# Block-causal attention and a hash-routed expert layer: q, k, V and weights loaded as bfloat16 through the GpSimd queue, and a new order of head pairs

## The chip, the cores and the metric

The kernel runs on one core of one Trainium2 chip. The metric is the device time of one execution in microseconds (us), lower is better. An execution has 336.15 us around a profiled span of 334.5 us; the other runs are given below.

## The reference, cut to what matters

```python
# q, k, v: [8, 8, 576, 64] float32
scores = (1 / sqrt(64)) * q @ k.T                       # per batch and head
scores = where(block_i >= block_j, scores, -1e9)        # blocks of 64 positions
attn = softmax(scores);  o = attn @ v
x = o.transpose(0, 2, 1, 3).reshape(4608, 512)          # one row per token
expert = token_ids * 2654435761 % 8                     # 4608 int64 ids
out[expert == e] = relu(x[expert == e] @ w1[e]) @ w2[e] # w1 [8,512,1024], w2 [8,1024,512]
```

## The kernel before, in words

The program has two parts: attention over 8 batches of 4 pairs of heads (32 pairs, `g`), and 8 experts over the tokens that a hash sends to them. The order of instructions on each engine is the order in which the program is written; nothing reorders it (a manual schedule). Each engine runs its own list in order, and waits where a tile that it needs is not ready.

**Loads.** `load_qk` and `load_v` fetch a batch of q, k and V as float32, on the SP queue (k of the first batch on ACT's), in runs of 256 to 1024 bytes. `cast_qk` turns q and k to bfloat16 on DVE (L175) and their last 64 rows on POOL (L180); `cast_v` and `cast_v4` do so for V on POOL (L188 to L199), into the tiles `vx` (six key tiles per head) and `v4` (the last 64 keys). The two weight matrices of an expert are loaded on POOL's queue with a cast to bfloat16 (`load_w1`, L555, and `load_w2`, L560).

**Attention.** For a pair `g`, `T_pair` transposes q and k on PE (eight 128 x 128 transposes, L236) and DVE copies them out of PSUM into `qkT` (L241); `T_rest` does the last 64 rows of all heads of a batch (L211, L217). `S_chunk` computes the scores of both heads of a pair in three chunks of 512 columns: matmuls of 64 rows, one head in the upper and one in the lower half of the array (L248, L260), and a small matmul that adds the mask (L270); ACT then takes the exponential of the chunk in one instruction (L294) into `pt`. `S_rest` does this for the last 64 keys (L302, L307). `PV` multiplies `pt` with V and a column of ones (15 matmuls per head, L331 and L336), and `norm` on DVE divides by the sum (L348, L351) into `xs`, which `write_x` stores to DRAM as rows of x (L362, L364): on SP for the first batches, on POOL from batch 5. The steps of one pass over `g` are the first chunk of `g`, the first half of `PV(g - 2)`, the second chunk, the second half and `norm(g - 2)`, the third chunk, the transposes of `g + 2`, and casts. There are two PSUM tiles for scores, one for `O`, and two for transposes.

**Routing.** `route` computes from the token ids each token's place in its expert's list, `rows`, `place_a` (one-hot tables on DVE, L499 and L502, multiplied on POOL, L505 and L508) and `place_b` (matmuls into the PSUM tile `pq`, which is one of the two for transposes, L518, and an addition on DVE, L521) turn it into the table `perm3` of rows. `place_a(j)` stands in pass 5 + 2j, `place_b(j)` in pass 8 + 2j.

**Experts.** `gather_x` fetches 128 rows of x by `perm3` (L567, POOL queue). The first three gathers of experts 0 and 1 need only batches 0 to 5 and stand in passes 27 and 28; the others wait for all of x. Each expert takes its tiles through `transpose_x` (L683, L684), `stage_a` or, for experts 0 and 1 in two parts, `stage_a_part` (L696 or L715, with a Relu on ACT), and `stage_b` (L729), whose results DVE copies out (L734) and POOL scatters (L736).

All transfers of the POOL queue use eight semaphores in turn, so that each issue waits until the transfer eight issues earlier has landed; the queue's transfers are issued in the order of POOL's list.

Of the kernel before, what the change touches and what calls it, by code (L numbers as in the profile page):

```python
# [19 lines left out]

B, H, S, D = 8, 8, 576, 64
E, DM, FF = 8, 512, 1024
# [15 lines left out]
def kernel(  # L38
# [26 lines left out]
    maskk = const.tile([P, 2, P], BF16, name="maskk")  # L65
    maskq = const.tile([P, P], BF16, name="maskq")
# [11 lines left out]


    nc.vector.memset(maskk[:], 0.0)  # L80
    nc.vector.memset(maskq[:], 0.0)
    for m in range(2):
        row = slice(64 * m, 64 * m + 1)
        nc.vector.memset(maskk[row, 0, 96:128], NEG)
        nc.vector.memset(maskk[row, 1, 32:64], NEG)
        nc.vector.memset(maskk[row, 1, 96:128], NEG)
        nc.vector.memset(maskq[row, :], 1.0)
# [3 lines left out]
    psT = att_ctx.enter_context(tc.tile_pool(name="psT", bufs=2, space=bass.MemoryType.PSUM))  # L91
# [9 lines left out]
    def load_qk(b, h0=0, h1=H, rest=True, main=True, engs=None):  # L101
        if b not in loaded:
            loaded[b] = [ld.tile([P, 36, D], F32, name="qf", tag="qf"),
                         ld.tile([P, 36, D], F32, name="kf", tag="kf"), None]
        for w, src in ((0, q), (1, k)):
            t = loaded[b][w]
            eng = engs[w] if engs else nc.sync
            if main and w == 0:
                eng.dma_start(
                    t[:, 4 * h0 : 4 * h1, :].rearrange("p (h c) d -> p h (c d)", c=4),  # L110
                    src[b, h0:h1, 0:512, :].rearrange("h (p c) d -> p h (c d)", c=4),
                )
            elif main:
                for r in range(2):
                    eng.dma_start(
                        t[:, 4 * h0 : 4 * h1, :].rearrange(
                            "p (h r c) d -> p h r (c d)", r=2, c=2)[:, :, r],
                        src[b, h0:h1, 256 * r : 256 * r + 256, :].rearrange("h (p c) d -> p h (c d)", c=2),
                    )
            if rest:  # L120
                for g in range(2):
                    eng.dma_start(
                        t[64 * g : 64 * g + 64, 32:36, :],
                        src[b, 4 * g : 4 * g + 4, 512:576, :].rearrange("h r d -> r h d"),
                    )

    def load_v(b):
        vf = ld.tile([P, 36, D], F32, name="vf", tag="vf")
        vm = vf[:, 0:32, :].rearrange("p (h r c) d -> p h r (c d)", h=H, r=2)
        for r in range(2):  # L130
            nc.sync.dma_start(
                vm[:, :, r, :],
                v[b, :, 256 * r : 256 * r + 256, :].rearrange("h (p c) d -> p h (c d)", c=2),
            )
        for m in range(2):
            nc.sync.dma_start(
                vf[64 * m : 64 * m + 64, 32:36, :],
                v[b, :, 512:576, :].rearrange("(r m) s d -> m s r d", m=2)[m],
            )
        loaded[b][2] = vf  # L140

    casted = {}
    vexts = []
    for z in range(2):
        vx = fix.tile([P, H, 6, D + 1], BF16, name=f"vx{z}")
        v4 = fix.tile([P, NP, 2, D + 1], BF16, name=f"v4{z}")
        nc.vector.memset(vx[:, :, :, D : D + 1], 1.0)
        nc.gpsimd.memset(v4[:], 0.0)
        for m in range(2):
            nc.vector.memset(v4[64 * m : 64 * m + 64, :, m, D : D + 1], 1.0)  # L150
        vexts.append((vx, v4))
    PTW = 1536
    pts, pt4s = [], []
    for z in range(3):
        pt = fix.tile([P, 2 * PTW + 64], BF16, name=f"pt{z}")
        nc.gpsimd.memset(pt[:, 2 * PTW :], 0.0)
        pts.append(pt)
    for z in range(2):
        pt4 = fix.tile([P, NP * 64 + 64], BF16, name=f"pt4{z}")
        nc.gpsimd.memset(pt4[:, NP * 64 :], 0.0)  # L160
        pt4s.append(pt4)
# [5 lines left out]
    def cast_qk(b, which, r0=0, r1=NP, rest=True):  # L167
        src = loaded[b][which]
        cb = casted.setdefault(b, {})
        if which not in cb:  # L170
            cb[which] = att.tile([P, 36, D], BF16, name="qb" if which == 0 else "kb",
                                 tag="qb" if which == 0 else "kb")
        dst = cb[which]
        if r1 > r0:
            nc.vector.tensor_copy(  # L175
                dst[:, 8 * r0 : 8 * r1, :].rearrange("p (r c m) d -> p r m c d", c=4, m=2),
                src[:, 8 * r0 : 8 * r1, :].rearrange("p (r m c) d -> p r m c d", c=4, m=2),
            )
        if rest:
            nc.gpsimd.tensor_copy(dst[:, 32:36, :], src[:, 32:36, :])  # L180

    def cast_v(b, pr):
        vf = loaded[b][2]
        vx, v4 = vexts[b % 2]
        hs = slice(2 * pr, 2 * pr + 2)
        vm = vf[:, 0:32, :].rearrange("p (h s) d -> p h s d", h=H)
        eng = nc.vector if b == 0 and pr < 2 else nc.gpsimd
        eng.tensor_copy(vx[:, hs, 0:4, 0:D], vm[:, hs])  # L188
        if pr % 2:
            return  # L190
        hs = slice(2 * pr, 2 * pr + 4)
        nc.gpsimd.tensor_copy(vx[0:64, hs, 4:6, 0:D], vm[0:64, hs, 0::2, :])
        nc.gpsimd.tensor_copy(vx[64:128, hs, 4:6, 0:D], vm[0:64, hs, 1::2, :])

    def cast_v4(b):
        vf = loaded[b][2]
        vx, v4 = vexts[b % 2]
        for m in range(2):
            nc.gpsimd.tensor_copy(  # L199
                v4[64 * m : 64 * m + 64, :, m, 0:D], vf[64 * m : 64 * m + 64, 32:36, :])  # L200

# [3 lines left out]
    def T_rest(b):  # L205
        qk = qkTs[b]
        tp = psT.tile([P, 8, P], BF16, name="tp", tag="tp")
        for w in range(2):
            src = casted[b][w]
            for x in range(2):  # L210
                nc.tensor.transpose(  # L211
                    out=tp[:, 2 * w + x, :],
                    in_=src[:, 32 + 2 * x : 34 + 2 * x, :].rearrange("p a d -> p (a d)"),
                    identity=identbf[:],
                )
        for w in range(2):
            nc.vector.tensor_copy(  # L217
                qk[:, :, w, 512:576].rearrange("p (g x) r -> p x g r", g=2),
                tp[:, 2 * w : 2 * w + 2, :].rearrange("p x (g r) -> p x g r", g=2),
            )  # L220

    def T_pair(g):
        b, pr = divmod(g, NP)
        if pr == 0:
            qkTs[b] = att.tile([P, NP, 2, S], BF16, name="qkT", tag="qkT")
        qk = qkTs[b]
        tp = psT.tile([P, 2, 512], BF16, name="tp", tag="tp")
        for w in range(2):
            src = casted[b][w]
            for c in range(4):  # L230
                s0 = (pr * 4 + c) * 2
                if w == 0:
                    o = tp[:, 0, :].rearrange("p (i c j) -> p c i j", i=4, c=4)[:, c]
                else:
                    o = tp[:, 1, 128 * c : 128 * c + 128]
                nc.tensor.transpose(  # L236
                    out=o,
                    in_=src[:, s0 : s0 + 2, :].rearrange("p a d -> p (a d)"),
                    identity=identbf[:],
                )  # L240
        nc.vector.tensor_copy(qk[:, pr, :, 0:512], tp[:])  # L241


    def mm_pair(b, pr, ps, o0, kt, q0, n, first=False):
        qk = qkTs[b]
        for m in range(2):
            rows = slice(64 * m, 64 * m + 64)
            nc.tensor.matmul(  # L248
                ps[:, m, o0 : o0 + n],
                lhsT=qk[rows, pr, 1, 128 * kt : 128 * kt + 128],  # L250
                rhs=qk[rows, pr, 0, q0 : q0 + n],
                start=first, stop=False,
            )

    def mm_c(b, pr, ps, o0, r):
        qk = qkTs[b]
        for x in range(2):
            for m in range(2):
                rows = slice(64 * m, 64 * m + 64)
                nc.tensor.matmul(  # L260
                    ps[64 * x : 64 * x + 64, m, o0 : o0 + 128],
                    lhsT=qk[rows, pr, 1, 256 * r + 128 * x : 256 * r + 128 * x + 64],
                    rhs=qk[rows, pr, 0, 256 * r : 256 * r + 128],
                    start=False, stop=False,
                )

    def mm_mask(ps, o0, c, n, last=False):
# [53 lines left out]
    def PV(g, m):  # L321
# [4 lines left out]
        if m == 0:  # L326
            ots[g] = psO.tile([P, 2, 512], F32, name="O", tag="O")
# [260 lines left out]
    for w in range(2):  # L588
        cast_qk(0, w, 0, 0)
# [258 lines left out]
```

## Time and profile before

| What | Value |
|---|---|
| Median of 3 runs | 339.33 us (337.66 to 340.61) |
| Profiled execution | 336.15 us, of it the span 334.5 us |
| PE, DVE, ACT, POOL busy | 276.5, 152.5, 142.5, 183.4 us |
| First and last Exp | 12.10 us start, 137.07 us end |
| Second expert stage of expert 0 starts | 178.39 us |
| Granted PE clock, mean | 0.951 |

PE is the matmul engine, PEld its loads of the stationary operand, DVE the vector engine, ACT the scalar engine, POOL is GpSimd. In a row of the profile `L294 ACT ACTIVATE pt<-ps ... x96 | 94.2, 1023 | 34.4 <-PE ps L270 34.2` the count is 96, the busy time 94.2 us, the mean of one 1023 ns, and the engine stood idle for 34.4 us just before them, most of it until PE had written `ps` at L270. In a row of the timeline the first number is the start in us, the second the duration of the merged stretch, and the bracket holds the idle time before it and what ended it. In a row of busy times by stretch come the stretch and its length, the busy time and number of instructions of PE, PEld, DVE, ACT and POOL, the granted clock, the share of the DMA engines, and GB/s.

### The profile page before, as it was taken

The page shows a single profiled execution, that of the slowest core. Times are in us where ns is not written, and L with a number is a line of the kernel's source. Part 1 is how long each engine was busy: PE and PEld are TensorE (multiplying, and loading weights), DVE is VectorE, ACT ScalarE, POOL GpSimd, SP SyncE. Part 2 cuts the span into 40 slices and gives each one's busy share as a digit, 9 for nine tenths or more (in the row PEclk, how much of TensorE's full clock was granted, in tenths as well). Part 3 has the DMA queues.
Part 4 walks back from the last instruction along what each step waited for, and adds up shares of the span by engine and source line. Part 5 has one row for each costly group of instructions (what it writes and reads, how often), then busy time and mean ns, then how long its engine had stood idle before and what let it go on. Part 6 is the DMA issues. An engine that isn't in the chain of part 4 may idle for free. (4 is left out here: it accounts for less than half of the span.)

```text
span 334.5 us, 7914 instructions
## 1 busy us (share of the span) xinstructions
PE 276.5 (83%) x3247; PEld 198.3 (59%) x3247; DVE 152.5 (46%) x342; ACT 142.5 (43%) x169; POOL 183.4 (55%) x265
## 2 busy tenths in 40 slices
PE   1559898989799899458589899799897996999990
PEld 0337676767577676347476594665745845759430
DVE  6487899888878775221011413033141130240430
ACT  1337888779687978304322050330501402406000
POOL 2185867687966529682487517447175075051451
PEclk9999999999989999959869999999999898999996
DMA  7999997979897975969189998677786586537231
GB/s 195 283 290 282 261 289 203 262 199 285 203 297 203 294 197 123 205 182 184 55 179 231 180 232 221 177 138 229 151 174 187 111 177 187 109 121 148 94 135 45
DMA packets 67044, 64.54 MB, mean 193 GB/s; under 512 B 17218, under 2 KB 61060, under 8 KB 64960
## 3 DMA queue, kind: packets, MB, share of 16 engines
q0 software_dynamic: 9248, 32.73, 41.1%
q1 hardware_dynamic: 55104, 30.12, 33.7%
q10 hardware_dynamic: 2656, 1.18, 1.4%
q8 instruction: 26, 0.43, 0.5%
q14 instruction: 10, 0.08, 0.1%
HBM read 67.15 MB, written 15.20 MB: 246 GB/s over the span
## 5 line engine op out<-in xcount | busy, mean ns | idle before, releaser
L294 ACT ACTIVATE pt<-ps 128x1024 bf16<-128x1024 f32 x96 | 94.2, 1023 | 34.4 <-PE ps L270 34.2
L701 ACT ACTIVATE hT<-hp 128x640 bf16<-128x640 f32 x48 | 33.6, 704 | 95.4 <-PE hp L696 78.6
L729 PE MATMUL yp<-w2b,hT 128*128 128x512 bf16 x320 | 70.2, 379 | 0.0
L696 PE MATMUL hp<-xT,w1b 128*128 128x320 bf16 x384 | 57.4, 309 | 9.1 <-ACT hT L701 8.2
L736 POOL DMA_INDIRECT out_dram<-ysb,perm x40 | 39.8, 995 | 38.6 <-DVE ysb L734 30.0
L696 PEld LDWEIGHTS <-w1b 128*128 128x128 bf16 x384 | 52.9, 145 | 13.5 <-issue 10.2
L567 POOL DMA_INDIRECT xg<-x_dram,perm x40 | 40.8, 1020 | 23.6 <-issue 12.9
L734 DVE COPY ysb<-yp 128x512 f32<-128x512 f32 x40 | 27.7, 692 | 55.9 <-PE yp L729 49.7
L729 PEld LDWEIGHTS <-hT 128*128 128x128 bf16 x320 | 31.1, 98 | 36.2
L684 DVE COPY xT<-tpx 128x512 bf16<-128x512 bf16 x40 | 15.6, 421 | 77.4 <-PE tpx L683 75.6
L331 PE MATMUL O<-vx,pt 128*128 128x65 bf16 x896 | 41.0, 199 | 6.7 <-DVE xs L351 5.4
L331 PEld LDWEIGHTS <-pt 128*128 128x128 bf16 x896 | 33.4, 101 | 10.2 <-issue 5.2
L248 PE MATMUL ps<-qkT 64*128 64x64 bf16 (+2 forms) x384 | 36.2, 269 | 3.0 <-ACT pt L294 2.6
L351 DVE TENSOR_TENSOR xs<-O,rs 128x320 bf16<-128x320 f32 x64 | 28.4, 486 | 1.1
L270 PE MATMUL ps<-maskq,maskk 64*128 64x64 bf16 (+1 forms) x256 | 28.1, 213 | 0.0
L188 POOL CAST vx<-vf 128x512 bf16<-128x512 f32 x30 | 21.1, 707 | 9.2 <-DMA vf<-in_v_dram 5.5
L719 ACT ACTIVATE hT<-hp 128x768 bf16<-128x768 f32 (+1 forms) x16 | 11.3, 704 | 31.7 <-PE hp L715 29.9
L241 DVE COPY qkT<-tp 128x1024 bf16<-128x1024 bf16 x32 | 22.0, 687 | 5.3 <-PE tp L236 4.6
L715 PE MATMUL hp<-xT,w1b 128*128 128x384 bf16 (+1 forms) x128 | 21.9, 338 | 2.3 <-DVE xT L684 2.3
L555 POOL DMA_DIRECT2D w1b<-in_moe_w_dram x8 | 4.8, 596 | 33.7 <-PE tpx L683 33.7
L683 PE MATMUL tpx<-identbf,xg 128*128 128x128 bf16 x160 | 14.7, 229 | 10.3 <-DMA xg<-x_dram,perm 6.6
L715 PEld LDWEIGHTS <-w1b 128*128 128x128 bf16 x128 | 17.4, 149 | 6.5 <-issue 2.9
(120 smaller groups left out, 289.6 us busy)
## 6 DMA issues: line engine op xcount, KB each, us to landing
vf<-in_v_dram SPq DMA_DIRECT2D x16, 512.0 KB, 5.9
w1b<-in_moe_w_dram POOLq DMA_DIRECT2D x8, 1024.0 KB
w2b<-in_moe_w_dram POOLq DMA_DIRECT2D x8, 1024.0 KB
qf<-in_q_dram SPq DMA_DIRECT2D x7, 1024.0 KB, 8.4
kf<-in_k_dram SPq DMA_DIRECT2D x14, 512.0 KB, 7.2
x_dram<-xs SPq DMA_DIRECT2D x20, 128.0 KB
x_dram<-xs POOLq DMA_DIRECT2D x12, 128.0 KB
qf<-in_q_dram SPq DMA_DIRECT2D x16, 64.0 KB, 6.3
```

The source lines that it names most:

```text
L248: nc.tensor.matmul(ps[:, m, o0 : o0 + n], lhsT=qk[rows, pr, 1, 128 * kt : 128 * kt + 128], rhs=qk[rows, pr, 0, q0 : q0 + n], start=first, ...
L270: nc.tensor.matmul(ps[:, m, o0 : o0 + 128 * n].rearrange("p (t h j) -> p t h j", h=2, j=16)[:, :, 0, :], lhsT=maskk[rows, c, :], rhs=maskq ...
L294: nc.scalar.activation(ptv[:, :, 512 * ch : 512 * ch + 512], ps[:], ACT.Exp, scale=SCALE)
L331: nc.tensor.matmul(O[:, t, :], lhsT=pt[:, m * PTW + o0 : m * PTW + o0 + 128], rhs=vx[:, h, i, :], start=(n == 0), stop=(n == t),)
L351: nc.vector.tensor_tensor(out=xs[:, :, 0:DM].rearrange("p t (d h k) -> p h t d k", d=4, h=H)[:, h], in0=O[:, m, :, 0:D].rearrange("p t (k ...
L567: nc.gpsimd.indirect_dma_start(out=xgs[g % (2 * G)][:], out_offset=None, in_=x_dram[0:n, :], in_offset=bass.IndirectOffsetOnAxis(ap=perm3[ ...
L696: nc.tensor.matmul(hp[:, t, 0:HC], lhsT=w1b[:, db, ft::NFT], rhs=xT[:, db, t * HC : (t + 1) * HC], start=(db == 0), stop=(db == NKT - 1),)
L701: nc.scalar.activation(hT[:, ft, :].rearrange("p (t n) -> p t n", t=2), hp[:, :, 0:HC], ACT.Relu)
L715: nc.tensor.matmul(hp[:, ft - f0, 0 : P * (t1 - t0)], lhsT=w1b[:, db, ft::NFT], rhs=xT[:, db, c], start=(db == 0), stop=(db == NKT - 1),)
L729: nc.tensor.matmul(yp[:], lhsT=hT[:, ft, tt * P : (tt + 1) * P], rhs=w2b[:, ft, :], start=(ft == 0), stop=(ft == NFT - 1),)
L734: nc.vector.tensor_copy(ysb[:], yp[:])
L736: ins = nc.gpsimd.indirect_dma_start(out=out[:, :], out_offset=bass.IndirectOffsetOnAxis(ap=perm3[:, gg : gg + 1], axis=0), in_=ysb[:], in ...
```

## The change

q, k and V are loaded by the POOL queue with a cast to bfloat16 in the transfer. q and k land in a layout in which a partition holds 18 successive rows of a head, for two heads (runs of 4608 bytes in DRAM); V lands directly in `vx`, which now has four key tiles of 96 columns per head, in three copies. All casts and the float32 tiles are gone. `T_group` replaces `T_pair` and `T_rest`: 18 transposes of 128 x 64 for half of a batch's q or k, and one strided copy. Heads of a pair are now `pr` and `pr + 4`. The scores use whole key tiles (`CHUNKS`, `mm_c` is gone). `PV` trails by one pair instead of two, after both first chunks; there are two `pt` instead of three. The PSUM of the transposes is one tile of two banks, and `place_b` uses the unused end of the next `O` tile. x rows keep their order, so `write_x` is one transfer per batch and one for the rest, and `vlo` is one column. Weights: w1 of experts 0 and 1 in passes 24 and 25, w2 in 26 and 30 (before: 25, 26, 29, and after the loop). `mo` has 8 buffers instead of 10. In the diff, code that both have is left out, and so are the memsets and the definitions of tiles.

```diff
+RUN = 18
+DV = 96
+NV = 3
...
-    psT = att_ctx.enter_context(tc.tile_pool(name="psT", bufs=2, space=bass.MemoryType.PSUM))
+    psT = att_ctx.enter_context(tc.tile_pool(name="psT", bufs=1, space=bass.MemoryType.PSUM))
...
+    def load_qk(b):
+        loaded[b] = []
+        for w, src in ((1, k), (0, q)):
+            t = ld.tile([P, 2, RUN, D], BF16, name="qb" if w == 0 else "kb",
+                        tag="qb" if w == 0 else "kb", bufs=3)
+            nc.gpsimd.dma_start(
+                t[:].rearrange("p m c d -> p m (c d)"),
+                src[b].rearrange("(m h) (j c) d -> (h j) m (c d)", m=2, c=RUN))
+            loaded[b].insert(0, t)
...
+    def load_v(b):
+        vx, v4 = vexts[b % NV]
+        for i in range(NT):
+            nc.gpsimd.dma_start(
+                vx[:, :, i, 0:D], v[b, :, 128 * i : 128 * i + 128, :].rearrange("h p d -> p h d"))
+        for m in range(2):
+            nc.gpsimd.dma_start(
+                v4[64 * m : 64 * m + 64, :, m, 0:D],
+                v[b, 4 * m : 4 * m + 4, 512:576, :].rearrange("r s d -> s r d"))
...
+    def T_group(b, n, act=False, pool=None):
+        if b not in qkTs:
+            qkTs[b] = [att.tile([P, NP, S], BF16, name=x, tag=x, bufs=3) for x in ("qT", "kT")]
+        w, z = divmod(n, 2)
+        c0, n = RUN // 2 * z, RUN // 2
+        pool, tag = pool or (psT, "tp")
+        tp = pool.tile([P, 16, P], BF16, name="tp", tag=tag)
+        for c in range(n):
+            for m in range(2):
+                nc.tensor.transpose(out=tp[64 * m : 64 * m + 64, c, :],
+                                    in_=loaded[b][w][:, m, c0 + c, :], identity=identbf[:])
+        (nc.scalar.copy if act else nc.vector.tensor_copy)(
+            qkTs[b][w][:].rearrange("p r (j c) -> p (r j) c", c=RUN)[:, :, c0 : c0 + n],
+            tp[:, 0:n, :].rearrange("p c r -> p r c"))
...
+    CHUNKS = [[(0, 0, 0, 512)], [(0, 1, 128, 448), (448, 0, 512, 64)], [(0, 2, 256, 320), (320, 3, 384, 192)]]
+    MASKS = [[0], [0], [0, 320]]
...
+        for n, (o0, kt, q0, w) in enumerate(CHUNKS[ch]):
+            mm_pair(b, pr, ps, o0, kt, q0, w, first=n == 0)
+        for o0 in MASKS[ch]:
+            mm_mask(ps, o0, last=o0 == MASKS[ch][-1])
+        pt = pts[g % 2]
...
-        for t in range(NT):
-            r0 = S * b + P * t
-            eng.dma_start(
-                x_dram[r0 : r0 + P, :].rearrange("(j c) d -> c j d", c=4), xs[:, t, :])
+        eng.dma_start(
+            x_dram[S * b : S * b + 512, :].rearrange("(t p) d -> p t d", p=P), xs[:, 0:NT, :])
...
-    def place_b(b):
+    def place_b(b, g):
         ohp, ohg = places.pop(b)
-        pq = psT.tile([P, 512], F32, name="pq", tag="tp")
+        ots[g] = psO.tile([P, 2, 512], F32, name="O", tag="O")
+        pq = ots[g][:, 0, 512 - 2 * NG :]
...
+    load_qk(0)
+    load_v(0)
+    load_qk(1)
+    T_group(0, 2)
+    T_group(0, 3, act=True, pool=(psO, "O"))
+    T_group(0, 0, pool=(psS, "ps"))
+    T_group(0, 1, act=True, pool=(psS, "ps"))
+
+    Ts = {g: [] for g in range(NPAIRS + 1)}
+    for b in range(1, B):
+        for n, g in zip((2, 3, 0, 1), (2, 2, 3, 3) if b == 1 else (4 * b - 3, 4 * b - 2, 4 * b - 1, 4 * b - 1)):
+            Ts[g].append((b, n))
...
+    loads[0].append((load_v, 1))
+    for b in range(2, B):
+        loads[4 * b - 7].append((load_qk, b))
+        loads[4 * b - 5].append((load_v, b))
+    for g, what in ((24, (load_w1, 0)), (25, (load_w1, 1)), (26, (load_w2, 0)), (30, (load_w2, 1))):
+        loads[g].append(what)
+    for g in range(NPAIRS + 1):
         b, pr = divmod(g, NP)
         live = g < NPAIRS
         if live:
             S_chunk(g, 0)
             S_chunk(g, 1)
+        if g in mids:
+            place_b(mids[g], g - 1)
+        if g >= 1:
+            PV(g - 1, 0)
+            PV(g - 1, 1)
+            norm(g - 1)
         if live:
             S_chunk(g, 2)
             if pr == 0:
                 S_rest(b)
+        for bn in Ts[g]:
+            T_group(*bn)
         for step in steps[g]:
             step()
+        if pr == 0 and b >= 1:
             write_x(b - 1)
+        for load, n in loads[g]:
+            load(n)
```

In the kernel after the change the transfers of q and k are line L103, those of V L121 and L124, the transposes and copies of `T_group` L156 and L158, the matmuls of `place_b` L407.

## The prediction

> **What bounds the kernel now.** I read, in this order: the page's busy shares and its 40 slices, the busy times by stretch, the timeline of ACT and PE inside the attention loop, and the timeline where attention ends. The chain of waits is of no help: it stops after the last two scatters.
>
> ```profile
> span 334.5 us, 7914 instructions
> PE 276.5 (83%) x3247; PEld 198.3 (59%) x3247; DVE 152.5 (46%) x342; ACT 142.5 (43%) x169; POOL 183.4 (55%) x265
> 33.20:137.10 103.90, 94.36 (x1963) 71.56 (x1961) 84.30 (x183) 84.22 (x92) 73.31 (x121) 0.98 0.88 234
> 137.10:178.40 41.30, 28.21 (x218) 22.74 (x216) 6.22 (x16) 10.45 (x15) 25.56 (x30) 0.79 0.73 161
> 178.40:334.50 156.10, 134.87 (x826) 91.47 (x823) 40.41 (x75) 34.41 (x50) 69.94 (x75) 0.96 0.65 159
> ```
>
> The three stretches (busy PE, PEld, DVE, ACT, POOL, clock, DMA share, GB/s) are 28 head pairs of attention, the seam to the experts, and the experts. The change leaves the experts' code as it is, so their 156 us stay. Ahead of them lies the fill (the first Exp starts at 12.10 and the fifth pair at 33.2).
>
> ```profile
> L294 ACT ACTIVATE pt<-ps 128x1024 bf16<-128x1024 f32 x96 | 94.2, 1023 | 34.4 <-PE ps L270 34.2
> 53.85 2.86 ACT L294 ACTIVATE pt<-ps 128x1024 bf16<-128x1024 f32 x3 [0.23 <-PE ps L270]
> ...
> 58.93 0.58 PE L518 MATMUL pq<-ohg,ohp 128*128 128x144 bf16 x5 [1.31 <-DVE qkT L241]
> ...
> 59.85 1.96 ACT L294 ACTIVATE pt<-ps 128x1024 bf16<-128x1024 f32 x2 [1.89 <-PE ps L270]
> ```
>
> In the loop ACT sets the pace: three Exps back to back take 2.86 and 0.23 passes before the next, 3.09 us a pair. Once per batch PE stands at L518 for a PSUM tile that DVE must empty, and ACT then waits 1.14 to 2.31 us. 103.9 us over 28 pairs is 3.71 each.
>
> ```profile
> 148.53 0.61 POOL L560 DMA_DIRECT2D w2b<-in_moe_w_dram x1
> 162.81 1.09 POOL L567 DMA_INDIRECT xg<-x_dram,perm  x1 [10.09 <-DMA x_dram<-xs]
> 165.66 0.61 PE L683 MATMUL tpx<-identbf,xg 128*128 128x128 bf16 x4 [3.18 <-DMA xg<-x_dram,perm]
> 178.39 0.81 PE L729 MATMUL yp<-w2b,hT 128*128 128x512 bf16 x3
> ```
>
> At the seam the last rows of x are written behind a weight load in the same queue, and the gathers wait 10.09 us for them. With other gaps and a cold clock (0.79) it is 41.3 us from the last Exp to the second expert stage, for 28.2 us of busy PE.
>
> **What the Trainium skill says.** "DMA: Bandwidth & Descriptors", SWDGE vs HWDGE vs iDMA: a transfer that casts must be issued by GpSimd, whose cores write its descriptors in software; Anatomy of one DMA adds "You can emit a lot of descriptors before the incremental cost shows up". The trace agrees as far as it goes: on POOL 64 rows (L364) took 573 ns and 128 rows (L555) 596. No row here has 1024 runs. "VectorE: DVE Perf Modes", What auto-detection actually checks: two 16-bit elements a cycle need step 1. The trace has only the fast case, L241: 1024 elements in 687 ns. "TensorE: Matmul & The Clock Gate", Part 3: matmuls in different column groups of the array run side by side. Eight quadrant matmuls of 128 columns (L260) start within 0.24 us at 53.28, against 0.55 us for the eight full transposes at 53.68, which agrees, though those differ in rows too.
>
> **The change, part by part.**
>
> Casts: four DVE casts a batch (757 and 841 ns) and about 7.4 us of POOL casts a batch (59.3 us in six groups) go. They were beside ACT's work; by themselves they save nothing but DVE room.
>
> Loads: all on POOL, eight transfers a batch; each waits for the one eight before it, which has long landed. Data: k and q in runs of 4608 bytes. By the DMA records the 128 packets of a weight load (2 MiB read, 8 packets an engine) last 6.5 us, with 625 ns for the shortest packet, so 1.18 MB is 3.6 at that pace and 2.8 at that packet's; V is 4608 runs of 256 bytes, at 19 ns each (the mean of the old 256-byte packets) over 16 engines 5.5 us. With the x rows some 13 us a batch, under the batch's 17: hidden. Descriptors: I take 0.54 us plus 0.9 ns a run, between the 0.4 of L364 against L555 and the 2.6 of L364 against L362 (737 ns, 128 rows in another order). A V transfer of 1024 runs is then 1.5 us (0.95 to 3.2), a batch 4.3 + 5.1 = 9.4 us of POOL (5120 runs); with the two L392/L395 products of 1.58 and a memset or two about 13.5 of 17 us. Hidden, with little to spare.
>
> Fill: k then q now land whole, at about 6 and 9 us; two groups of transposes and a copy on ACT (1152 elements; by ACT's 512, 768 and 1024 rows 1.13 us) put the first Exp near 12.3 instead of 12.10. No step gain there.
>
> Transposes: eight plus one of 58 ns a pair become 18 with 64 columns. If they overlap as L260's do, 0.6 us a pair, if not 1.0; I take 0.6. Their copy reads PSUM with a step of 128 elements, so one element a cycle: 1152 / 0.96 = 1200 plus the 150 ns that L351 has over its 320 elements, 1.35 us, four a batch. Bounds: 0.75 (L241's rate) and 1.6.
>
> Scores: 28 matmuls a pair become 18 (the third chunk 0.68 to about 0.40 us). PV stays at 30 (0.57 per 15). PE per pair: 0.36 + 0.36 + 1.14 + 0.40 + 0.6 = 2.86 us, under ACT.
>
> Order: PV now trails by one pair, behind both first chunks. From the second chunk's start: PV ends at 1.50, the third chunk at 1.90, its Exp runs 2.10 to 3.12, and the next second chunk, which needs that PSUM tile, starts at 3.17. So 3.17 a pair; 3.53 with S_rest; place_b adds 0.3, but its wait for the shared tile is gone (four or five stalls, 8.5 us).
>
> What is late next: the last two transposes of a batch (q) stand at the end of the pair before their use, with one PSUM tile between them. Third chunk ends 1.90; transposes to 2.5; copy, behind the 1.13 us norm on DVE, to about 4.1; transposes to 4.7; copy to 6.1; only then the next batch's first chunk, whose second starts at 6.6 to 7.1. So 3.9 us more than a plain pair, with ACT idle, at seven boundaries, and 2.3 more at the first, where k's two groups share a pair.
>
> Sum: a middle batch is 3.53 + 2.86 + 3.17 + 3.2 + 3.9 = 16.7; with place_b in two pairs (four batches) 17.3; the first 19.0; the last 12.8. 19.0 + 2 x 16.7 + 4 x 17.3 + 12.8 = 134.4. The same recurrence gives the loop before 100.9 where the trace has 103.9, so times 1.03: 138.4. From 12.3 the last Exp ends at 150.7, against 137.07: 13.6 us later.
>
> Seam: w1 and w2 go out from pair 24 on, three loads of 6.5 us in the 21 us before pair 30 and the fourth after; x's last rows are written with nothing before them, and the late gathers land while PE does the early parts. What remains: PV and norm 2.7; two times tiles 1.9 (155.19 to 157.09) and 32 matmuls 5.35; two times 1.24 (173.60 to 174.84) and 3.6. 26.9 us instead of 41.3: 14.4 gained. Against it, a pause of 3.7 us of norm (L348, released by nothing the trace names) near the end of attention before may recur: 1.5. Small edits (route, rows, masks, memsets) lie beside loads: nothing either way, at most 1 us.
>
> Together 13.6 - 14.4 + 1.5 = +0.7 us. The profiled execution is 336.15 (1.65 around its span); on the median of 339.33 that is 340.0.
>
> **Rivals.** (1) POOL becomes the bound, the case on the slow side: descriptors of V at L121. A batch fits as long as 4.3 + 5.12 s + 4.2 stays under 17.3, s below 1.7 ns a run. At 2.0 PE waits 8 us in all (348), at 2.6 31 us (371). For it: L362's 737 ns, the indirect transfers' 1020 ns for 128 rows, the eight short runs per partition. Against it: 596 ns for 128 runs. (2) The column halves don't overlap: 18 transposes in 1.0 us; plain pairs 3.26, boundaries 0.4 more: 154.0 rather than 147.1 before the 3 per cent, 347. For it: all 58 ns rows are full width. (3) The strided copy keeps L241's rate: 0.75 us, the boundary stall falls to 2.5 us and the batch to 16: 10 us earlier, 329.5. Against it: step 128, and runs of nine with odd starts.
>
> **How the numbers follow.** The forecast has 0.45, with 333 to 347 of its own from the bounds (clock, fill, 1.5 us of pause, w loads): of it 0.07 faster, 0.25 within, 0.13 slower, at the 1% that a measurement of this kernel can tell. Rival 1 has 0.27 (0.26 slower, 0.01 within), rival 2 0.16 (0.12 slower, 0.04 within), rival 3 0.12, faster. Faster 0.19, within 0.30, slower 0.51. The range reaches from rival 3 to most of rival 1: 330 to 366.
>
> **What would show it.** Right: an ACT wait of about 4 us at each batch's first Exp and none at L407's matmuls; copies at L158 near 1.35 us; L121 issues near 1.5 us; the last Exp near 150, and no 10 us wait at the gathers. Wrong: PE waiting at PV for V's transfers (rival 1), L156 taking 1 us a group (2), copies under 0.9 us (3), or a seam still over 35 us.

## The result and the profile after

The changed kernel took 361.79 us (median of four runs, 359.34 to 364.22), the kernel before beside it 339.97: a ratio of 1.067, 95% interval 1.056 to 1.077. It is slower by some 22 us. The profiled execution took 362.32 us with a span of 360.7, against 336.15 and 334.5. Two later comparisons gave ratios of 1.070 (1.061 to 1.078) and 1.077 (1.072 to 1.082).

The page of the changed kernel, first the span and the busy shares, then the granted TensorE clock in 40 slices of 9 us (9 is 90% or more):

```profile
span 360.7 us, 7588 instructions
PE 276.8 (77%) x3215; PEld 205.7 (57%) x3215; DVE 141.0 (39%) x289; ACT 144.0 (40%) x171; POOL 167.1 (46%) x215
PEclk9859976889778598886569999999999999999995
```

PE was busy as long as before (276.5) with fewer matmuls, and its share fell from 83% to 77%. The clock row says why the sum didn't shrink: in 16 of the first 21 slices, the attention and the seam, 5 to 8 tenths stand where full speed would be 9.

The busy times by stretch, in the columns of the prediction (span, busy PE, PEld, DVE, ACT, POOL, clock, DMA share, GB/s), are the fifth pair's first Exp to the end of the last Exp, then to the second expert stage, then to the end:

```profile
34.75:172.51 137.76, 100.33 (x1873) 78.65 (x1869) 76.17 (x141) 83.61 (x91) 62.68 (x88) 0.80 0.92 136
172.51:206.08 33.57, 25.43 (x193) 20.89 (x194) 4.99 (x13) 10.68 (x16) 13.84 (x15) 0.80 0.24 61
206.08:360.70 154.62, 132.11 (x826) 90.83 (x823) 40.42 (x75) 34.03 (x49) 69.06 (x75) 0.98 0.65 160
```

The 28 pairs took 137.76 us instead of 103.90. DVE and POOL have less to do than before, ACT the same; the clock is 0.80 instead of 0.98. The seam shrank from 41.30 to 33.57, the experts stayed.

Three groups of the page answer questions of the prediction (busy, mean ns of one, idle time before and its releaser):

```profile
L195 ACT ACTIVATE pt<-ps 128x1024 bf16<-128x1024 f32 x96 | 93.2, 1024 | 63.5 <-PE ps L177 62.8
L121 POOL DMA_DIRECT2D vx<-in_v_dram x32 | 28.6, 913 | 0.5 <-DMA vx<-in_v_dram 0.4
L158 DVE COPY qT<-tp 128x1152 bf16<-128x1152 bf16 x15 | 20.4, 1357 | 7.6 <-PE tp L156 7.6
```

An Exp takes as long as before; the waits of the Exps for PE grew from 34.2 to 62.8 us. A V transfer of 1024 runs holds POOL for 913 ns, and the strided copy takes 1357.

The timeline at a batch's end, all engines, shows both halves of what happened:

```profile
123.83 1.01 PE L156 MATMUL tp<-identbf,kb 128*64 128x128 bf16 x18
124.77 0.39 PE L167 MATMUL ps<-qT,kT 64*128 64x512 bf16 x2
...
126.51 0.58 PE L232 MATMUL O<-vx,pt 128*128 128x65 bf16 x14 [0.48 <-DVE acc L410]
...
127.89 0.69 PE L156 MATMUL tp<-identbf,kb 128*64 128x128 bf16 x18
...
128.52 0.39 PE L167 MATMUL ps<-qT,kT 64*128 64x512 bf16 x2
...
130.89 0.69 PE L156 MATMUL tp<-identbf,qb 128*64 128x128 bf16 x18
131.68 1.35 DVE L158 COPY qT<-tp 128x1152 bf16<-128x1152 bf16 x1
133.08 0.69 PE L156 MATMUL tp<-identbf,qb 128*64 128x128 bf16 x18 [1.50 <-DVE qT L158]
133.81 1.36 DVE L158 COPY qT<-tp 128x1152 bf16<-128x1152 bf16 x1 [0.78 <-PE tp L156]
...
135.23 0.61 PE L167 MATMUL ps<-qT,kT 64*128 64x512 bf16 x2 [1.45 <-DVE qT L158]
...
135.99 1.94 ACT L195 ACTIVATE pt<-ps 128x1024 bf16<-128x1024 f32 x2 [3.90 <-PE ps L177]
136.30 0.95 PE L232 MATMUL O<-vx,pt 128*128 128x65 bf16 x14
```

The two q groups stand behind one PSUM tile, PE waits 1.50 and 1.45 us for the copies, and ACT waits 3.90. After that stand-still the same instructions are slower: two score matmuls of 512 columns take 0.61 us instead of 0.39, half a PV 0.95 instead of 0.58. The stretch behind another stall, the one whose Exp starts at 50.94, has a clock of 0.50 for 10 us. But 3.4 us at 0.50 also follow a single, shorter wait inside a pair, that of PV for DVE's addition into `acc`:

```profile
49.50:59.60 10.10, 8.13 (x109) 6.12 (x109) 3.58 (x9) 5.18 (x6) 6.32 (x8) 0.50 1.10 151
63.34 0.93 PE L232 MATMUL O<-vx,pt 128*128 128x65 bf16 x14 [1.41 <-DVE acc L410]
63.10:66.40 3.30, 3.06 (x52) 2.76 (x53) 1.29 (x4) 0.52 (x2) 2.97 (x4) 0.50 0.15 8
```

By the profiler's record of the granted clock, the 28 pairs hold 54.8 us at 0.50, and the rest is at 1.00. Of these, 41.0 us lie in six stretches that begin in a batch's stall or just behind it (the first of the seven stalls has none), and 13.8 us in three that begin so at single waits inside pairs, of 1.41, 2.00 and 1.66 us.

In the seam, PE's timeline and then DVE's:

```profile
175.46 1.01 PE L544 MATMUL tpx<-identbf,xg 128*128 128x128 bf16 x8 [1.33 <-DVE xs L252]
179.75 0.58 PE L544 MATMUL tpx<-identbf,xg 128*128 128x128 bf16 x4 [3.28 <-DVE xT L545]
180.85 7.87 PE L576 MATMUL hp<-xT,w1b 128*128 128x384 bf16 x32 [0.52 <-DVE xT L545]
...
191.25 5.42 PE L576 MATMUL hp<-xT,w1b 128*128 128x384 bf16 x32 [0.52 <-DVE xT L545]
```

```profile
179.27 0.76 DVE L545 COPY xT<-tpx 128x512 bf16<-128x512 bf16 x2 [3.96 <-DMA x_dram<-xs]
```

The gathers' wait for x, 10.09 us before, is 3.00 us now. But the first xT copy waits 3.96 us for the last write of x, which it doesn't read, and the first expert part takes 7.87 us where the second, with the same 32 matmuls, takes 5.42.

### The profile page after: what moved, and what is told of

Same layout as the page of the kernel before. It is cut to its first block, busy times and chain, and to the rows that moved or that the text cites. A ratio compares the mean times of both kernels' runs of the same rounds, so it can differ in the third digit from the quotient of the medians.

```text
span 360.7 us, 7588 instructions
## 1 busy us (share of the span) xinstructions
PE 276.8 (77%) x3215; PEld 205.7 (57%) x3215; DVE 141.0 (39%) x289; ACT 144.0 (40%) x171; POOL 167.1 (46%) x215
## 5 line engine op out<-in xcount | busy, mean ns | idle before, releaser
L195 ACT ACTIVATE pt<-ps 128x1024 bf16<-128x1024 f32 x96 | 93.2, 1024 | 63.5 <-PE ps L177 62.8
L167 PE MATMUL ps<-qT,kT 64*128 64x512 bf16 (+4 forms) x320 | 42.9, 352 | 26.1 <-ACT pt L195 12.9
L557 PEld LDWEIGHTS <-w1b 128*128 128x128 bf16 x384 | 52.2, 144 | 11.4 <-issue 10.4
L232 PEld LDWEIGHTS <-pt 128*128 128x128 bf16 x896 | 41.0, 114 | 9.0 <-issue 5.7
L167 PEld LDWEIGHTS <-kT 64*128 64x128 bf16 x320 | 14.4, 103 | 37.7 <-issue 20.3
L249 DVE RECIPROCAL rs<-O 128x10 f32<-128x10 f32 x32 | 7.1, 221 | 56.6 <-PE O L237 54.4
L252 DVE TENSOR_TENSOR xs<-O,rs 128x320 bf16<-128x320 f32 x64 | 28.4, 486 | 1.1
L121 POOL DMA_DIRECT2D vx<-in_v_dram x32 | 28.6, 913 | 0.5 <-DMA vx<-in_v_dram 0.4
L392 POOL TENSOR_TENSOR ohg<-ohs,vhi 128x360 bf16<-128x360 bf16 x8 | 6.3, 783 | 43.3 <-DVE ohs L389 25.8
L158 DVE COPY qT<-tp 128x1152 bf16<-128x1152 bf16 x15 | 20.4, 1357 | 7.6 <-PE tp L156 7.6
L177 PE MATMUL ps<-maskq,maskk 64*128 64x64 bf16 x256 | 22.6, 212 | 0.0
L158 DVE COPY kT<-tp 128x1152 bf16<-128x1152 bf16 x15 | 20.3, 1355 | 5.4 <-PE tp L156 4.2
```

Source lines behind the costliest of these rows:

```text
L121: nc.gpsimd.dma_start(vx[:, :, i, 0:D], v[b, :, 128 * i : 128 * i + 128, :].rearrange("h p d -> p h d"))
L158: (nc.scalar.copy if act else nc.vector.tensor_copy)(qkTs[b][w][:].rearrange("p r (j c) -> p (r j) c", c=RUN)[:, :, c0 : c0 + n], tp[:, 0: ...
L167: nc.tensor.matmul(ps[:, m, o0 : o0 + n], lhsT=kT[rows, pr, 128 * kt : 128 * kt + 128], rhs=qT[rows, pr, q0 : q0 + n], start=first, stop=F ...
L195: nc.scalar.activation(ptv[:, :, 512 * ch : 512 * ch + 512], ps[:], ACT.Exp, scale=SCALE)
L232: nc.tensor.matmul(O[:, t, :], lhsT=pt[:, m * PTW + o0 : m * PTW + o0 + 128], rhs=vx[:, h, i, 0 : D + 1], start=(n == 0), stop=(n == t),)
L252: nc.vector.tensor_tensor(out=xs[:, :, 0:DM].rearrange("p t (d h k) -> p h t d k", d=4, h=H)[:, h], in0=O[:, m, :, 0:D].rearrange("p t (k ...
```

## The experiments

**Theory A:** the double transpose group at each batch's end stalls PE and ACT for about 4 us, and the granted clock, halved after such a stand-still, stretches the pairs that follow. **Theory B:** the stalls are all that the order costs; the low clock comes from elsewhere. **Theory C:** PV's waits on the acc addition slow the pairs and lower the clock. **Theory D,** added later: without the stalls, the copies and PV's waits set the pace. "The loop" below is the stretch from the fifth pair's first Exp to the end of the last.

The kernel before took 326.03 us on the chip of the first four edits ("the first chip" below), and 344.52 and 338.79 beside the next two sets, which ran on two other chips; on the first chip the experts alone were 10 us shorter than in the profile above (144.5 for 154.6). So kernels of different sets are compared by their ratio to the kernel before, and by stretches, not by their microseconds.

**Transpose groups spread over four pairs.**

```diff
-(2, 2, 3, 3) if b == 1 else (4 * b - 3, 4 * b - 2, 4 * b - 1, 4 * b - 1)
+(1, 1, 2, 2) if b == 1 else (4 * b - 5, 4 * b - 4, 4 * b - 3, 4 * b - 2)
```

> The changed kernel with each batch's four transpose groups one or two head pairs earlier (at pairs 4b-5, 4b-4, 4b-3, 4b-2 instead of 4b-3, 4b-2, 4b-1, 4b-1), so that no two of them share the last pair of a batch. Theory A (the double group stalls PE and ACT for about 4 us at seven boundaries, and the idle TensorE is then granted half its clock, which stretches the pairs that follow): the 3.5 to 4.3 us waits at each batch's first Exp go, some 24 us in all; the clock between the fifth pair and the last Exp rises from 0.80 to over 0.95, worth another 12 to 15 us; 320 to 327 us, faster than both kernels. Theory B (the stall is all there is to it, the low clock comes from elsewhere, such as the small V packets or PE waiting inside the pairs): the clock stays near 0.80 and only the stalls go, about 338 us.

341.3 us, ratio 1.045 (1.038 to 1.052). That gains less than either theory asked: the loop took 127.48 us with a clock of 0.87, and five of the seven batch starts still waited, 17.0 us in sum. The waits of PE in that stretch (us in total, times, longest) name a new cause:

```profile
PE tp L156 <- DMA kb<-in_k_dram: 15.5, 5, 4.7
```

The groups had been moved ahead of the landing of their loads. The edit swapped one stall for another, and so doesn't decide between A and B.

**place_b after the first half of PV.**

```diff
-        ots[g] = psO.tile([P, 2, 512], F32, name="O", tag="O")
...
-        if g in mids:
-            place_b(mids[g], g - 1)
         if g >= 1:
             PV(g - 1, 0)
+            if g in mids:
+                place_b(mids[g], g - 1)
             PV(g - 1, 1)
```

The first line goes because PV now opens the `O` tile that place_b uses.

> The changed kernel with the five matmuls of place_b put after the first half of PV instead of ahead of it, so that PV no longer waits for DVE's addition into acc in the same PSUM tile. Theory A (boundary stall and clock): the waits of PV on the acc addition (5.9 us over eight pairs) go, but these are pairs whose other waits remain; 356 to 361 us, clock still near 0.80 in the loop. Theory C (PV's wait on the addition is what slows the pairs and lets the clock fall): 5.9 us of wait and most of the low clock go, under 350 us.

340.11 us, ratio 1.041 (1.036 to 1.046), loop 127.78 us, clock 0.85. The waits on acc didn't go: 4.7 us in eight, since the second half of PV writes into the same tile and now waited in place of the first. Most of the gain over the unedited kernel's loop (6.4 of 10.0 us) lay in the last six pairs, where no place_b is left, so it isn't this edit's own. The microseconds expected were worked out for a slower chip. The run is inconclusive.

**Both edits.**

> Both edits together: transpose groups spread over four pairs, place_b after the first half of PV. Theory A: as with the spread groups alone and up to 5 us less, 316 to 325 us. Theory B: 333 us. Theory C: the same as place_b moved alone less the stalls, under 325 us with the clock restored by the place_b edit.

336.13 us, ratio 1.027 (1.019 to 1.036), loop 119.98 us, clock 0.93. The waits for k (17.8 us) and for acc (5.7 us) both remain. No theory had this; the edits were at fault.

**The stall left in place, PE kept at work in it.** `warm` issues six matmuls of 128x512 on zeros into the next `O` tile; nothing reads them.

```diff
...
         for bn in Ts[g]:
             T_group(*bn)
+            if pr == NP - 1 and g < NPAIRS - 1 and b >= 0 and bn[1] in (0, 1):
+                warm(g, 6 if bn[1] == 0 else 6)
```

> The changed kernel with six matmuls of 512 columns on zeros added behind each of the two q transpose groups at a batch's end; they fill PE's idle time there and nothing reads what they write. The stall of ACT at the batch's first Exp stays. Theory A (PE's idle time there costs the clock): the loop's clock rises from 0.80 to over 0.92, the stall stays near 3.9 us, pairs at half clock of 4.4 us become 3.2 to 3.5; 346 to 351 us. Theory B (the clock comes from elsewhere): the clock stays near 0.80, 361 to 364 us.

332.79 us, ratio 1.021 (1.014 to 1.027). The loop took 118.44 us with a clock of 1.00; the batch starts still waited 3.67 to 3.80 us each, 26.5 in sum against 26.8. This is what A expects, and B is out: nothing was taken away, 84 matmuls were added, and the ratio fell from 1.067 to 1.021.

To have it beside the unedited kernel on one chip, both ran again later:

> The changed kernel, unedited, once more, so that the two single edits that follow stand beside it on one chip. From two earlier chips: ratio 1.05 to 1.08, 136 to 138 us from the fifth pair's first Exp to the end of the last, clock 0.80 to 0.82 in that stretch.

> Again the changed kernel with six matmuls on zeros behind each of the last two transpose groups of a batch, now beside the unedited kernel. If PE's idle time is what costs the clock on any chip: stalls of 3.8 us as before, clock 0.95 or more, 118 to 121 us for the stretch of 28 pairs, 15 to 19 us less than the unedited kernel. If the first chip of the edits granted its clock otherwise: clock under 0.90 and less than 10 us gained.

Unedited 364.01 us, ratio 1.077 (1.072 to 1.082); with the added matmuls 350.68, ratio 1.038 (1.030 to 1.047). The loops, unedited and then edited:

```profile
34.98:168.99 134.01, 96.38 (x1873) 75.52 (x1869) 76.00 (x141) 83.27 (x91) 62.59 (x88) 0.84 0.94 140
```

```profile
33.36:159.13 125.77, 103.40 (x1945) 73.48 (x1941) 75.77 (x141) 82.97 (x91) 62.43 (x88) 0.95 1.00 149
```

PE did 7 us more and the stretch was 8.2 us shorter; the medians are 13.3 us apart, since the unedited execution profiled was the fastest of its five. Both are less than the 15 to 19 us expected: one pair near the end took 10.88 us there, and the clock reached 0.95, not 1.00. PE's timeline at a batch's end of the edited kernel, where the added matmuls stand at L248, and ACT's at another:

```profile
102.56 1.47 PE L248 MATMUL O<-wz,identbf 128*128 128x512 bf16 x6 [0.23 <-DVE xs L260]
103.96 0.69 PE L158 MATMUL tp<-identbf,qb 128*64 128x128 bf16 x18
104.58 1.47 PE L248 MATMUL O<-wz,identbf 128*128 128x512 bf16 x6
106.11 0.39 PE L169 MATMUL ps<-qT,kT 64*128 64x512 bf16 x2
```

```profile
124.47 2.85 ACT L197 ACTIVATE pt<-ps 128x1024 bf16<-128x1024 f32 x3 [3.80 <-PE ps L179]
```

ACT stands as long as before, but the score matmuls after it take 0.39 instead of 0.61.

**The unedited kernel beside the next three.**

> The changed kernel itself, unedited, next to the runs it is to be compared with, since the kernel before took 340 us on the chip of the first comparison and 326 us on the chip of the edits. If the edits so far gained what their ratios say, this run's ratio to the kernel before is again 1.05 to 1.08, with the loop's clock near 0.80. If the chip made the difference, the ratio is near 1.04 and the place_b edit alone gained nothing.

367.16 us, ratio 1.070 (1.061 to 1.078), loop 136.70 us, clock 0.82. As expected; so the earlier edits' ratios hold against it.

**Spread groups with q and k loaded three pairs earlier.**

```diff
-        loads[4 * b - 7].append((load_qk, b))
+        loads[max(4 * b - 10, 0)].append((load_qk, b))
```

> The changed kernel with the transpose groups spread over four pairs, as before, and the q and k loads put three pairs earlier (end of pair 4b-10 instead of 4b-7), so that k's first group no longer waits for its landing, which cost PE 15.5 us when only the groups were spread. Theory A (stall at the boundary, and the clock that falls with it): waits at the batches' first Exps under 5 us in sum instead of 26.8, the clock over 0.95, and 28 pairs at 3.3 to 3.6 us, 93 to 101 us from the fifth pair to the last Exp instead of 137.8; ratio to the kernel before 0.95 to 0.98. Theory D (without the stalls the copies and PV's waits on DVE set the pace): over 108 us, ratio 1.00 or more.

341.50 us, ratio 0.994 (0.990 to 0.997), 25.7 us less than the unedited kernel. No batch start from the fifth pair on waits at all. The loop took 109.26 us, so D is nearer than A: the clock is 0.95, and PE's waits on acc grew from 5.9 to 9.6 us. Three of these eight waits are followed by 3.4 us at a clock of 0.50, which is all the low clock that the loop has.

```profile
PE O L232 <- DVE acc L410: 9.6, 8, 1.4
```

**The same, with place_b behind both halves of PV.**

```diff
             PV(g - 1, 0)
             PV(g - 1, 1)
+            if g in mids:
+                place_b(mids[g], g - 1)
             norm(g - 1)
```

> The same as the run before it, with place_b's five matmuls put after both halves of PV, so that the next work in that PSUM tile is the following pair's PV, about 2 us later. PV's waits on the acc addition (4.7 to 5.9 us over eight pairs so far) should end. If they were on the path: 3 to 5 us faster than the run before it. If ACT paces these pairs anyway: no difference that can be measured.

As above, the line that opens place_b's own tile goes too. 327.91 us, ratio 0.952 (0.948 to 0.957): 13.6 us less, not 3 to 5. The waits on acc are gone, and with them the rest of the low clock:

```profile
34.46:129.34 94.88, 79.50 (x1850) 64.01 (x1849) 74.53 (x141) 82.74 (x92) 65.94 (x92) 1.00 1.29 188
```

94.88 us for 28 pairs is 3.39 each. The 9.6 us of waits were worth 14.4 us of loop, because they too cost clock. C was right in this much: PV's waits on acc lower the clock too.

**The same, with xs in the pool that stays open,** so that xT lies elsewhere.

```diff
-        xfix.append(fix.tile([P, 5, DM], BF16, name=f"xs{z}"))
+        xfix.append(const.tile([P, 5, DM], BF16, name=f"xs{z}"))
```

> The same as the run before it, with the three xs tiles allocated in the pool that stays open, so that the experts' xT tiles no longer lie where the last write of x still reads. The wait of the first xT copy on the landing of x (3.96 us in the changed kernel, 10 us where attention ended earlier) should go, with up to that much of the stretch from the last Exp to the second expert stage; 3 to 9 us faster than the run before it. If the late gathers set the end of that stretch, 0 to 2 us.

320.72 us, ratio 0.926 (0.919 to 0.932). From the last Exp to the second expert stage 29.18 us instead of 36.40, which is all of the 7.2 us gained. DVE's timeline there:

```profile
132.77 0.80 DVE L544 COPY xT<-tpx 128x512 bf16<-128x512 bf16 x2 [0.82 <-PE tpx L543]
```

The wait for x's landing (5.93 us in the run before it) is gone. So it came from memory that xT took over from xs. The low clock there stays: the first expert part takes 7.48 us, the second 5.42.

**place_b behind PV alone,** the rest as changed (on the chip where the unedited kernel took 364.01 us).

> The changed kernel with only place_b moved behind both halves of PV, transposes and loads untouched. Theory A (the stalls at the boundary keep the clock low): the 6 us of PV's waits on the acc addition go, with the stalls and a clock of 0.80 to 0.85 kept; 4 to 8 us faster than the unedited kernel. Theory C (the waits inside the pairs keep it low): clock over 0.90, 12 us or more faster.

354.04 us, ratio 1.045 (1.038 to 1.052), 10 us under the unedited kernel, more than A's 4 to 8. But the two profiled executions differ by 3.0 us (spans 354.8 and 357.8), the loop by 3.3, and with the stalls still there (26.9 us in sum) the clock is 0.79. The stalls alone suffice to hold it down, as A says, though one wait of 2.61 us inside a late pair is followed by 17 us of half clock too; how much this edit is worth by itself lies between 3 and 10 us.

**Added matmuls in the first pairs of the fastest version.** Six matmuls on zeros after the first four transpose groups, and six between the two groups of pair 1 and of pair 2.

> The fastest version so far (spread groups, early q and k loads, place_b after PV, xs tiles apart from xT; ratio 0.9255 to the kernel before), with six matmuls on zeros added after the first transposes and in the two pairs that hold both groups of batch 1, where PE still stands 1.5 us and ran at half clock for 14 us. The first four pairs took 20.1 us in that version; at full clock 15.5 to 18; ratio 0.91 to 0.92. If the low clock there has another cause: ratio 0.925 to 0.93.

315.11 us, ratio 0.931 (0.924 to 0.939). The first four pairs took 16.1 us instead of 20.1, as expected, but the ratio is no better than the version without (intervals overlap): the later 28 pairs took 98.03 us at a clock of 0.95 instead of 95.04 at 1.00. Whether the added matmuls brought that about or the chip did is open. Both versions beat the kernel before by 7%.

## Why the prediction was right or wrong

The forecast was 340.0, the measurement 361.8: inside the range of 330 to 366, but by luck. The range went up that far for rival 1, and rival 1 fell; the 333 to 347 of the main argument miss it. The clock, which made most of the gap, stands in none of the rivals. Against the profiled execution the sum was 336.85 and the time 362.32, 25.5 us apart: first Exp at 14.09 instead of 12.3 (1.8, of it some 1.4 because k and q were there at 7.5 and 10.4 us, not at 6 and 9), loop from the first Exp to the end of the last 158.4 instead of 138.4 (20.0), seam 33.6 instead of 28.4 with the pause in it (5.2), experts 154.6 instead of 156.1 (-1.5).

**Right.** The stall at the boundary: 3.53 to 4.34 us at seven batch starts for a forecast of 3.9. The strided copy: 1.36 us for 1.35, so rival 3 fell. Transposes: 0.63 us a group at full clock from the first to the next work (127.89 to 128.52) for 0.6; they took 0.94 (123.83 to 124.77) only at half clock, so rival 2 fell. L407 waits no more. The seam did shrink, and the gathers' 10 us wait went down to 3.0. That the casts gave nothing back fits these sums, but no run takes them alone.

**Wrong but harmless.** A V transfer's descriptors took 0.91 us for a forecast of 1.5, and its four larger ones a batch 3.7, so rival 1, which had carried the slow side of the range, fell. What the prediction had quoted from the Trainium skill, "DMA: Bandwidth & Descriptors", Anatomy of one DMA, that many descriptors can be emitted before the cost shows, held better than the value taken: 0.67 us for 256 runs (L124) and 0.91 for 1024 are 0.3 ns a run. (The POOL sum had 5.1 where 5120 runs at 0.9 ns give 4.6, and rival 2 starts from 147.1 where 12.3 and 134.4 give 146.7; neither slip matters.) The data took longer than thought: by the DMA records V's packets carry 128 bytes and last 32 ns each, 9.2 us a batch over 16 engines for a forecast of 5.5, and k and q, 512 packets of 2304 bytes at 205 ns, 6.5 us for a forecast of 2.8 to 3.6. The forecast had set the 1.18 MB of k and q that land against the 2 MiB that a weight load reads; such a load lands half of that, and at its pace k and q are 7.3 us, not 3.6. With loads a batch and more ahead nobody waited for the data in the changed kernel's loop; in the first run with spread groups PE waited for k.

**Wrong by most of the gap:** the step "The same recurrence gives the loop before 100.9 where the trace has 103.9, so times 1.03: 138.4". It priced every PE duration at the clock of before, 0.98, in an order that it had just given seven stand-stills of 4 us. With PE kept busy in these, the stretch from the first Exp to the end of the last was 137.6 us (14.37 to 152.01) on the first chip, 0.8 from the sum, at a clock of 1.00. On the chip where the unedited kernel ran beside it, it fell from 154.7 to 144.7, still 6.3 above the sum, at 0.95. So the sum of stalls and durations was nearly right in total, and most of what it left out is the clock: 13.3 us between the medians on that chip (364.01 against 350.68).

The profile of before already had the effect. Its clock is 0.50 for 3.4 us behind a single wait of 1.73 us at L518, and for 10 us behind the pause of 3.75 us where attention ends, in which the first expert part is slower than the second, with as many matmuls (5.39, at 157.09):

```profile
148.31 7.05 PE L715 MATMUL hp<-xT,w1b 128*128 128x384 bf16 x32 [0.51 <-DVE xT L684]
```

The prediction named this "a cold clock (0.79)" and gave it no price in the loop.

The Trainium skill, "TensorE: Matmul & The Clock Gate", Part 1, states that the clock is halved after at least one idle window of about 3.4 us, and that the window runs freely. The prediction had drawn on Part 3 of that page. The trace agrees in the value, 0.50, but not in the idle time that it takes. At the batch ends PE's idle pieces were 1.46 to 1.53 and 1.45 us. The only work between them was transposes, and Part 4 of that page says that these do not count as busy in the same way; counted so, the gap from the end of the last score matmuls (130.96) to the next (135.23) is 4.3 us. But the clock fell as well in the wait of 1.41 us that ends at 63.34, with ordinary matmuls up to it. So a gap of 3.4 us is not needed here. How little idle time suffices stays open; that ordinary matmuls in the gaps keep the clock is shown.

**Two errors inside that sum that cancelled.** "So 3.17 a pair": at full clock a plain pair took 2.76, three Exps without a wait, since the 30 PV matmuls took 1.01 us from start to the next work (100.24 to 101.25 in the edited kernel) instead of 1.14, and the third chunk came in time. And "place_b adds 0.3, but its wait for the shared tile is gone" was half right: the wait moved. PV, next in that tile, waited for the addition on DVE, 5.9 us over eight pairs. With the clock at 1.00 (the added matmuls, first chip), batches without place_b took 16.1 us for 17.2 (16.7 times 1.03), those with it 18.5 on the mean for 17.8.

**Wrong by 5 us:** "What remains ... 26.9 us". It missed that the first xT copy must wait for the last write of x (3.3 us of PE, shown by the xs edit) and that the first expert part would run in part at half clock (7.87 against 5.42), though that of before had done so. Without the first, 29.18 us; take off the 2.1 us that the slow first part still costs there (7.48 against 5.42) and it is 27.1, the forecast. The pause priced at 1.5 did not come back at the last norm, but one like it stands in pair 26, where ACT idles for 1.9 us with its scores there and PE waits 2.00 us behind it; its cause stays open.

## What to carry to other kernels

When an order gives TensorE a regular stand-still of some microseconds, price the work after it at half the clock: here 26 us of stalls cost another 8 us in the loop of the profiled executions, 13 between the medians. Single waits of 1.4 us cost clock too, though not each time. In such a program, putting two instructions' outputs into one PSUM tile turns the reader of the first into a wait for the writer of the second, and a pool that is closed and reopened does the same to memory that a DMA still reads; look for both whenever an edit "removes" a wait. A change that is slower as a whole may hold a faster kernel: with the groups spread, their loads earlier, place_b behind PV and xs kept apart, the same change runs at 0.926 of the kernel before.

## What the runs showed of the hardware

Six matmuls of 512 columns on zeros in each gap (1.47 us each time) raised the clock of the loop from 0.84 to 0.95 on one chip, and it was 1.00 with them on another. Eight waits of 0.4 to 1.4 us in 109 us went with a clock of 0.95, three of them followed by 3.4 us at 0.50; without them it was 1.00. In the loops of all these traces the clock is 0.50 or 1.00 and nothing between, and every stretch at 0.50 that begins there lasts 3.41 us or a multiple of it, up to 20.5. A packet of 128 bytes of a casting transfer took 32 ns, more than one of 256 bytes without a cast in the kernel before (19 ns). The experts, the same code in all, took from 144.5 to 161.0 us, so ratios on one chip are what can be compared.
